# Decode kernel with cached attention: keys brought in by transposing DMAs in place of TensorE transposes and copies

## The chip, the cores and the metric

The kernel runs on one core of a Trainium2 chip. The metric is the device time of one execution in microseconds (us). Beside it the profile has a span, from the first to the last recorded instruction, and names of engines: PE is TensorE, with PEld for its weight loads, DVE is VectorE, ACT is ScalarE, POOL is GpSimd, and SP is SyncE, which issues all the DMAs of this kernel.

## The reference

Four sequences (B = 4) decode one token each through the same two layers twice: attention over cached keys and values, and a gated MLP. Keys and values have 8 heads of 4096 rows of 128 bf16 numbers; each key head serves 4 query heads.

```python
def _A_ref(x, k_cache, v_cache, wq, wo):
    q = (x @ wq).reshape(B, 1, 32, 128).transpose(0, 2, 1, 3)
    k = repeat(k_cache, 4, axis=1); v = repeat(v_cache, 4, axis=1)
    p = softmax(einsum("bhqd,bhkd->bhqk", q, k) * 128 ** -0.5)
    o = einsum("bhqk,bhkd->bhqd", p, v)
    return o.transpose(0, 2, 1, 3).reshape(B, 1, 4096) @ wo
def _B_ref(x, w_gate, w_up, w_down):
    return (gelu(x @ w_gate) * (x @ w_up)) @ w_down
x = x + _A_ref(layernorm(x), k_cache, v_cache, wq, wo)
x = x + _B_ref(layernorm(x), w_gate, w_up, w_down)
x = x + _A_ref(layernorm(x), k_cache, v_cache, wq, wo)
x = x + _B_ref(layernorm(x), w_gate, w_up, w_down)
```

Both attention layers use the same caches and weights. The caches are 33.6 MB each, the weights 13.9 MB.

## The kernel before

The loop at line 371 goes over the four sequences ("batches"). In a batch the first attention layer, its MLP and the scores of the second attention layer are computed; the second layer's values for that batch follow in the next batch's turn, beside the next batch's keys. So keys are read from HBM once per batch, and values twice. The last batch's second-layer values, and the last MLP for all four batches together, form the tail after the loop (lines 470 to 488).

Keys: keys(b, kvh) at line 253 fills one of 8 resident tiles kt (pool ktp, 1 MB each, head dimension on the partitions), which stay until the second layer's scores of the batch have read them. It loads two raw tiles k_t of 512 KB through load_kv (line 124; a ring of 6 buffers, KV_BUFS, that keys and values share), turns every 128 x 128 block on PE (line 262, 32 to a head) into a PSUM tile tp, and evac (line 246) copies each group of 8 blocks to kt, two copies of five on ACT (line 249), three on DVE (line 251).

Scores: scores (line 270) multiplies the queries, placed in a sparse tile zq, with the resident keys, 8 matmuls a head (line 276), and collects 4 heads in one PSUM tile sc. softmax (line 281) works on such a group of 4 heads with DVE, POOL and ACT, and turn (line 305) transposes its result pr to pT. set_queries (line 161) puts the queries of a batch into zq.

Values: values (line 315) loads two tiles v_t of 512 KB for a head and multiplies them with pT (line 328); its finish transposes the result back (line 337), and DVE writes it to OT_bf (lines 342 and 343). out_proj (line 184) multiplies by wo.

Order: tc.manual_schedule (line 349) keeps the instructions of PE and SP as they are written. Both engines take their instructions in that order, so an SP instruction that waits holds every DMA written after it. In the loop, V(kvh, p) is a value head of the first layer, W() one of the second layer of the batch before (an "old" head), and O() the finish of the oldest head still open. Before the change the order of a batch is: keys 0; turns of the old softmaxes (batch 0: the second half of wq and the q projection); keys 1 to 7, with the scores of head k written after the keys of head k+1, two old heads after the scores of heads 1 and 2, the softmax of heads 0 to 3 after the scores of head 3, and values 0 to 2 between keys 6, keys 7 and the last scores; the softmax of heads 4 to 7; values 3; an old head; then values 4 to 7 with the output projection, and the norms, the MLP (ffn, line 202) and the q projection of the second layer with the other five old heads between their steps; last the second layer's scores, line 465 on, head by head, with their softmaxes. Batch 0 also loads wo before values 3 (line 429) and the three MLP weights after values 7 (line 448).

Of the kernel before, what the change touches and what calls it, by code (L numbers as in the profile page):

```python
# [9 lines left out]
BF16 = mybir.dt.bfloat16  # L10
# [5 lines left out]
P = 128  # L16
# [3 lines left out]
CH = 16  # L20
TB = 8
GH = 4
# [5 lines left out]
def kernel(  # L28
# [16 lines left out]
    nc = tc.nc  # L45
    B, Sq, D = A_x.shape
    _, Hkv, Sk, Dh = A_k_cache.shape
# [8 lines left out]
    NT = C // CH  # L56
    NKB = 8
    NCC = C // NKB
    CT = NCC // NT
# [8 lines left out]
    ktp = ctx.enter_context(tc.tile_pool(name="ktp", bufs=Hkv))  # L68
# [11 lines left out]
    ident_bf = const.tile([P, P], BF16, name="ident_bf")  # L80
# [42 lines left out]
    def load_kv(cache, b, kvh, t, name):  # L123
        tl = kvin.tile([P, CH, Dh], BF16, name=name, tag="kv")
        rows = slice(t * CH * P, (t + 1) * CH * P)
        dq.dma_start(out=tl[:], in_=cache[b, kvh, rows].rearrange("(p c) d -> p c d", p=P))  # L126
        return tl
# [33 lines left out]
    def set_queries(z, b):  # L161
        nc.vector.tensor_copy(out=z[:, :, ZP:ZP + rep],
                              in_=q1_bf[:, b].rearrange("p (k h) -> p k h", h=rep))

    def q_proj(b0, nb, dst, parts):
        bs = slice(b0, b0 + nb)
        hp = Hq // parts
        for part in range(parts):
            qps = ps_misc.tile([P, nb, hp], FP32, name="qps", tag="misc")
            for i in range(hp):  # L170
                m = part * hp + i
                for k in range(KD):
                    nc.tensor.matmul(qps[:, :, i], lhsT=wq_sb[:, k, m * Dh:(m + 1) * Dh],  # L173
                                     rhs=xn_bf[:, bs, k], start=(k == 0), stop=(k == KD - 1))
            if nb == 1:
                nc.vector.tensor_copy(
                    out=dst(part, hp),
                    in_=qps.rearrange("p o (k h) -> p (o k) h", h=rep))
            else:
                nc.vector.tensor_copy(out=dst(part, hp), in_=qps[:])  # L180
# [60 lines left out]


    KT = {}
    evac_ctr = [0]

    def evac(out_ap, in_ap):
        evac_ctr[0] += 1
        if evac_ctr[0] % 5 in (1, 3):
            nc.scalar.copy(out=out_ap, in_=in_ap)  # L249
        else:  # L250
            nc.vector.tensor_copy(out=out_ap, in_=in_ap)  # L251

    def keys(b, kvh):

        kt = ktp.tile([P, NKB, NCC, P], BF16, name="kt", tag="kt")
        KT[kvh] = kt
        for t in range(NT):
            kn = load_kv(A_k_cache, b, kvh, t, "k_t")
            for g in range(CH // TB):
                tp = ps_tp.tile([P, TB // CT, CT, P], BF16, name="tp", tag="tp")  # L260
                for i in range(TB):
                    nc.tensor.transpose(tp[:, i // CT, i % CT, :], kn[:, g * TB + i, :],  # L262
                                        ident_bf[:, :])
                k0 = g * TB // CT
                evac(kt[:, k0:k0 + TB // CT, t * CT:(t + 1) * CT, :], tp[:])

    def new_scores():
        return ps_sc.tile([P, NCC * P], FP32, name="sc", tag="sc")
# [1 line left out]
    def scores(sc, kvh, zq):  # L270

        s = kvh % GH
        for kbp in range(2):
            off = ZP - rep * (2 * s + kbp)
            for j in range(4):
                nc.tensor.matmul(sc[32 * j:32 * j + 32, :], lhsT=zq[:, kvh, off:off + 32],  # L276
                                 rhs=KT[kvh][:, 2 * j + kbp].rearrange("p c k -> p (c k)"),
                                 start=(s == 0 and kbp == 0), stop=(s == GH - 1 and kbp == 1),
                                 skip_group_check=True)

# [24 lines left out]
    def turn(soft):  # L305

        pr, rden = soft
        ptp = ps_tp.tile([P, NCC, P], BF16, name="ptp", tag="tp")
        for cc in range(NCC):
            nc.tensor.transpose(ptp[:, cc, :], pr[:, cc, :], ident_bf[:, :])  # L310
        pT = pTp.tile([P, NCC, P], BF16, name="pT", tag="pT")
        nc.vector.tensor_copy(out=pT[:], in_=ptp[:])
        return pT, rden

    def values(b, kvh, prob, o_bf):

        pT, rden = prob
        s = kvh % GH  # L320
        ot = ps_ot.tile([P, 2, 2 * Dh], FP32, name="ot", tag="ot")
        for t in range(NT):
            v = load_kv(A_v_cache, b, kvh, t, "v_t").rearrange(
                "p (j b c) d -> p j c b d", j=4, b=2, c=CT)
            for cl in range(CT):
                cc = t * CT + cl
                for j in range(4):
                    nc.tensor.matmul(  # L328
                        ot[32 * j:32 * j + 32, 0].rearrange("p (b d) -> p b d", b=2),
                        lhsT=pT[:, cc, 32 * j:32 * j + 32], rhs=v[:, j, cl],  # L330
                        start=(cc == 0), stop=(cc == NCC - 1))
        os = osp.tile([P, 2, Dh], FP32, name="os", tag="os")
        nc.scalar.copy(out=os.rearrange("p b d -> p (b d)"), in_=ot[:, 0])  # L333

        def finish():
            for k in range(2):
                nc.tensor.transpose(ot[:, 1, k * P:(k + 1) * P], os[:, k, :], ident_f[:, :])  # L337
            od = grp.tile([P, rep], FP32, name="od", tag="od")

            src = ot[:, 1, 8 * s:]  # L340
            sel = bass.AP(src.tensor, src.offset, [src.ap[0], [1, rep], [132, 2], [32, 4]])
            nc.vector.tensor_reduce(out=od[:], in_=sel, axis=AX.XY, op=ALU.add)  # L342
            nc.vector.tensor_tensor(out=o_bf[:, b, kvh * rep:(kvh + 1) * rep], in0=od[:],  # L343
                                    in1=rden[:, s], op=ALU.mult)

        return finish
# [24 lines left out]
    for b in range(B):  # L371
        z1 = zq1[b % 2]
        old = list(range(Hkv)) if b > 0 else []
        rest = []

        def V(kvh, prob):
            rest.append(values(b, kvh, prob, OT_bf))

        def W():
            if old:  # L380
                kvh = old.pop(0)
                rest.append(values(b - 1, kvh, prob2[kvh // GH], OT2_bf))

        def O():
            if rest:
                rest.pop(0)()

        if b > 0:
            set_queries(z1, b)
        sc = new_scores()  # L390
        keys(b, 0)
        if b == 0:
            dq.dma_start(out=wq_sb[:, :, hq0:], in_=wq_dram[:, :, hq0:])
            q_proj(0, B, lambda part, hp: q1_bf[:, :, part * hp:(part + 1) * hp], 4)
            set_queries(z1, 0)
        else:
            prob2 = [turn(soft2[0])]
        keys(b, 1)
        if b > 0:
            prob2.append(turn(soft2[1]))  # L400
        scores(sc, 0, z1)
        keys(b, 2)
        scores(sc, 1, z1)
        W()
        keys(b, 3)
        O()
        scores(sc, 2, z1)
        W()
        keys(b, 4)
        O()  # L410
        scores(sc, 3, z1)
        soft1 = softmax(sc)
        sc = new_scores()
        keys(b, 5)
        p0 = turn(soft1)
        scores(sc, 4, z1)
        V(0, p0)
        keys(b, 6)
        O()
        scores(sc, 5, z1)  # L420
        V(1, p0)
        keys(b, 7)
        O()
        scores(sc, 6, z1)
        V(2, p0)
        scores(sc, 7, z1)
        soft1 = softmax(sc)
        if b == 0:
            dma_weights("wo")
        V(3, p0)  # L430
        O()
        W()
        O()
        p1 = turn(soft1)
        V(4, p1)
        O()
        out_proj(b, 1, OT_bf, range(0, 4))
        V(5, p1)
        O()
        out_proj(b, 1, OT_bf, [4])  # L440
        V(6, p1)
        O()
        out_proj(b, 1, OT_bf, [5])
        V(7, p1)
        O()
        out_proj(b, 1, OT_bf, [6])
        if b == 0:
            dma_weights("wg", "wu", "wd")
        W()
        O()  # L450
        out_proj(b, 1, OT_bf, [7])
        for _ in ffn(b, 1):
            W()
            O()
        for _ in layer_norm(b, 1):
            W()
            O()
        while old:
            W()
            O()  # L460
        q_proj(b, 1, lambda part, hp: zq2[:, part * GH:(part + 1) * GH, ZP:ZP + rep], 2)
        while rest:
            O()
        soft2 = []
        for g in range(2):
            sc = new_scores()
            for s in range(GH):
                scores(sc, g * GH + s, zq2)
            soft2.append(softmax(sc))
# [49 lines left out]
```

## Time and profile before

| | us |
|---|---|
| two runs of the kernel before | 386.70 and 391.99, median 389.35 |
| the profiled execution | 388.58 |
| its span | 386.8 |

The mean granted clock of TensorE in the profiled execution is 0.706 of full speed. From the groups of instructions, beside those that are shown further down:

| line, engine, what | count | busy us |
|---|---|---|
| 328 PE, values | 1024 | 61.0 |
| 337 PE, turning the results back | 128 | 39.9 |
| 276 PE, scores of the second layer | 256 | 23.4 |
| 333 ACT, copying the results | 64 | 23.8 |
| 192 PE, output projection | 640 | 21.4 |

A group's row has the line, the engine, the operation, out<-in with shapes, the count, then busy us and mean ns of one, then the idle time before them on their engine and what ended it. A row of the timeline has the start and the length in us, the engine and the line, and the number of instructions that were merged; a bracket tells how long the engine had stood idle before and what released it. Matmuls overlap, so the lengths of PE rows that follow each other overlap too, and starts are the safer guide. A row of the DMA issues has the number of DMAs, the KB of one (1 KB is 1024 bytes; MB are millions of bytes), and the us from issue to landing. Windows show for each stretch the busy time of every engine, the granted clock and what the DMA engines did.

### The profile page before, as it was taken

Reading aid. Unit: us, or ns where it says so; the run is one execution under the profiler, and the core shown is the slowest. Engines: PE = TensorE matmul, PEld = TensorE weight load, DVE = VectorE, ACT = ScalarE, POOL = GpSimd, SP = SyncE. Lnnn points to the kernel's source line nnn. Section 1 sums busy time; section 2 is a strip of 40 time slices with the busy share of each in tenths; the row PEclk is TensorE's granted clock in tenths of the full one; section 3 lists DMA queues with packets and bytes.
Section 4 is the critical chain, followed back from the end, with each engine's and each line's share of the span. In section 5 each row is a group of like instructions: output and inputs, shape, how many; then the busy total and the mean of one; then the engine's idle time right before and its main releaser. Section 6 shows DMA issues by size and latency. Waiting matters only on the chain.

```text
span 386.8 us, 11139 instructions
## 1 busy us (share of the span) xinstructions
PE 277.7 (72%) x4900; PEld 198.9 (51%) x4900; DVE 135.7 (35%) x528; ACT 90.0 (23%) x154; POOL 14.0 (4%) x38
## 2 busy tenths in 40 slices
PE   0699704845987868879967577878967688796855
PEld 0686602645566525565755345664745355553535
DVE  0546411132454421341735211434653213313132
ACT  1236310100353411100634311101644211002100
POOL 0000000000100000000100000001000000001000
PEclk9999875555798965555989955557999655556555
DMA  7989999996189999970698999861899999704900
GB/s 284 407 314 341 380 350 408 403 374 252 55 288 407 363 407 407 401 290 3 228 402 309 366 403 352 339 219 55 282 410 406 409 395 382 276 8 156 386 5 2
DMA packets 35745, 115.29 MB, mean 298 GB/s; under 512 B 3176, under 2 KB 9072, under 8 KB 35696
## 3 DMA queue, kind: packets, MB, share of 16 engines
q1 hardware_dynamic: 35696, 114.58, 78.6%
q8 instruction: 38, 0.62, 0.6%
q14 instruction: 11, 0.09, 0.1%
HBM read 114.56 MB, written 0.00 MB: 296 GB/s over the span
## 4 chain that ended last, share of the span: by engine, by line
PE 47%; DMA 25%; DVE 15%; issue 6%; ACT 3%; SPq 2%; POOL 2%; DVEq 0%; POOLq 0%; ACTq 0%
DMA k_t<-in_A_k_cache_dram 10%; PE ot L328 10%; DMA v_t<-in_A_v_cache_dram 10%; PE tp L262 9%; PE ot L337 7%; PE sc L276 6%; DMA wd_sb<-in_B_w_down_dram 5%; PE qps L173 5%; PE yT L192 4%; ACT pr L294 2%; PE hg L210 2%; PE hu L227 2%; DVE kt L251 2%; SPq L126 2%; DVE od L342 2%
## 5 line engine op out<-in xcount | busy, mean ns | idle before, releaser
L262 PE MATMUL tp<-ident_bf,k_t 128*128 128x128 bf16 x1024 | 74.1, 232 | 16.4 <-DMA k_t<-in_A_k_cache_dram 10.9
L328 PE MATMUL ot<-v_t,pT 128*32 128x256 bf16 x1024 | 61.0, 371 | 32.7 <-DMA v_t<-in_A_v_cache_dram 26.3
L262 PEld LDWEIGHTS <-k_t 128*128 128x128 bf16 x1024 | 65.6, 105 | 29.7 <-DMA k_t<-in_A_k_cache_dram 15.6
L251 DVE COPY kt<-tp 128x1024 bf16<-128x1024 bf16 x76 | 51.3, 688 | 50.8 <-PE tp L262 50.2
L249 ACT COPY kt<-tp 128x1024 bf16<-128x1024 bf16 x52 | 52.3, 1012 | 59.8 <-PE tp L262 59.6
L328 PEld LDWEIGHTS <-pT 128*32 128x32 bf16 x1024 | 28.9, 116 | 50.1 <-DMA v_t<-in_A_v_cache_dram 19.1
L333 ACT COPY os<-ot 128x256 f32<-128x256 f32 x64 | 23.8, 372 | 132.5 <-PE ot L328 132.5
L342 DVE TENSOR_REDUCE od<-ot 128x4 f32<-128x32 f32 x64 | 12.0, 187 | 93.9 <-PE ot L337 93.6
L337 PE MATMUL ot<-ident_f,os 128*128 128x128 f32 x128 | 39.9, 412 | 2.1 <-ACT os L333 2.1
L192 PEld LDWEIGHTS <-wo_sb 128*128 128x128 bf16 x640 | 23.0, 107 | 16.7 <-issue 16.3
L192 PE MATMUL yT<-OT_bf,wo_sb 128*128 128x1 bf16 (+1 forms) x640 | 21.4, 166 | 10.8 <-DVE OT_bf L343 10.7
L337 PEld LDWEIGHTS ot<-ident_f,os 128*128 128x128 f32 x128 | 17.5, 192 | 21.2 <-issue 16.4
L173 PE MATMUL qps<-xn_bf,wq_sb 128*128 128x1 bf16 (+1 forms) x640 | 18.9, 166 | 12.0 <-DVE xn_bf L157 10.1
L294 ACT ACTIVATE pr<-sc,nb 128x512 bf16<-128x512 f32 x16 | 11.0, 688 | 69.3 <-DVE am L290 67.7
L173 PEld LDWEIGHTS <-wq_sb 128*128 128x128 bf16 x640 | 18.1, 104 | 12.8 <-DVE xn_bf L157 10.5
L276 PE MATMUL sc<-kt,zq_128 128*32 128x512 bf16 x256 | 23.4, 545 | 0.0
L283 DVE TENSOR_REDUCE m<-sc 128x1 f32<-128x512 f32 x16 | 11.0, 689 | 20.4 <-PE sc L276 20.3
L288 POOL PARTITION_ALL_REDUCE gm<-am x16 | 6.2, 388 | 301.2 <-DVE am L285 301.2
L276 PEld LDWEIGHTS <-zq_128 128*32 128x32 bf16 x256 | 8.5, 131 | 13.9 <-issue 12.4
L210 PE MATMUL hg<-xn_bf,wg_sb 128*128 128x1 bf16 (+1 forms) x280 | 8.3, 166 | 8.0 <-DVE xn_bf L157 8.0
L210 PEld LDWEIGHTS <-wg_sb 128*128 128x128 bf16 x280 | 7.9, 104 | 9.4 <-DVE xn_bf L157 6.7
L310 PE MATMUL ptp<-ident_bf,pr 128*128 128x128 bf16 x64 | 7.4, 248 | 6.4 <-ACT pr L294 6.1
(118 smaller groups left out, 157.5 us busy)
## 6 DMA issues: line engine op xcount, KB each, us to landing
v_t<-in_A_v_cache_dram SPq DMA_DIRECT2D x128, 512.0 KB, 6.3
k_t<-in_A_k_cache_dram SPq DMA_DIRECT2D x64, 512.0 KB, 6.2
wq_sb<-in_A_wq_dram SPq DMA_DIRECT2D x2, 2048.0 KB, 10.8
wo_sb<-in_A_wo_dram SPq DMA_DIRECT2D x1, 4096.0 KB, 19.5
wg_sb<-in_B_w_gate_dram SPq DMA_DIRECT2D x1, 1792.0 KB, 11.2
wu_sb<-in_B_w_up_dram SPq DMA_DIRECT2D x1, 1792.0 KB, 15.4
wd_sb<-in_B_w_down_dram SPq DMA_DIRECT2D x1, 1792.0 KB, 20.1
x_bf<-in_A_x_dram SPq DMA_DIRECT2D x1, 4.0 KB
```

Of the source, the lines that this page charges most:

```text
L173: nc.tensor.matmul(qps[:, :, i], lhsT=wq_sb[:, k, m * Dh:(m + 1) * Dh], rhs=xn_bf[:, bs, k], start=(k == 0), stop=(k == KD - 1))
L192: nc.tensor.matmul(OP["y"][:, :, dk], lhsT=wo_sb[:, i, dk * P:(dk + 1) * P], rhs=o_bf[:, bs, i], start=(i == 0 and dk == 0), stop=(i == Hq ...
L210: nc.tensor.matmul(hg[:, m, :], lhsT=wg_sb[:, k, m * P:(m + 1) * P], rhs=xn_bf[:, bs, k], start=(k == 0), stop=(k == KD - 1))
L249: nc.scalar.copy(out=out_ap, in_=in_ap)
L251: nc.vector.tensor_copy(out=out_ap, in_=in_ap)
L262: nc.tensor.transpose(tp[:, i // CT, i % CT, :], kn[:, g * TB + i, :], ident_bf[:, :])
L276: nc.tensor.matmul(sc[32 * j:32 * j + 32, :], lhsT=zq[:, kvh, off:off + 32], rhs=KT[kvh][:, 2 * j + kbp].rearrange("p c k -> p (c k)"), st ...
L294: nc.scalar.activation(out=pr.rearrange("p c k -> p (c k)"), in_=sc[:], func=ACT.Exp, bias=nb[:, 0:1], scale=scale, accum_out=ls[:])
L328: nc.tensor.matmul(ot[32 * j:32 * j + 32, 0].rearrange("p (b d) -> p b d", b=2), lhsT=pT[:, cc, 32 * j:32 * j + 32], rhs=v[:, j, cl], star ...
L333: nc.scalar.copy(out=os.rearrange("p b d -> p (b d)"), in_=ot[:, 0])
L337: nc.tensor.transpose(ot[:, 1, k * P:(k + 1) * P], os[:, k, :], ident_f[:, :])
L342: nc.vector.tensor_reduce(out=od[:], in_=sel, axis=AX.XY, op=ALU.add)
```

## The change

keys no longer loads raw tiles, turns and copies them. It issues one transposing DMA from SP for a head, from the cache in HBM to the resident tile. The 4096 rows of a head are viewed as 256 rows of 16 consecutive keys (2048 elements); the DMA writes, for each of the 16 keys in such a row, a run of 256 elements in each of the 128 partitions. So the tile has the shape 128 x 16 x 256 in place of 128 x 8 x 4 x 128, a new helper kcols picks the 512 columns for a matmul of the scores, and the index of the chunk of pT in values goes from t * CT + cl to cl * NT + t to match. The raw tiles k_t, the transposes of line 262 and evac are gone; the 6 buffers of load_kv serve values alone.

The order of a batch changes with it. All eight key DMAs are issued first (in batch 0 the second half of wq behind the first of them), then the q projection of batch 0 or the turns of the old softmaxes, set_queries, the scores of all heads with the two softmaxes, and only then value heads. No old head stands ahead of value head 7 now; in batches 1 to 3 all eight come from there on, three of them between the second norm and the q projection. wo stays between values 2 and 3.

```diff
     KT = {}
-    evac_ctr = [0]
-
-    def evac(out_ap, in_ap):
-        evac_ctr[0] += 1
-        if evac_ctr[0] % 5 in (1, 3):
-            nc.scalar.copy(out=out_ap, in_=in_ap)
-        else:
-            nc.vector.tensor_copy(out=out_ap, in_=in_ap)
 
     def keys(b, kvh):
 
-        kt = ktp.tile([P, NKB, NCC, P], BF16, name="kt", tag="kt")
+
+        kt = ktp.tile([P, CH, Sk // CH], BF16, name="kt", tag="kt")
         KT[kvh] = kt
-        for t in range(NT):
-            kn = load_kv(A_k_cache, b, kvh, t, "k_t")
-            for g in range(CH // TB):
-                tp = ps_tp.tile([P, TB // CT, CT, P], BF16, name="tp", tag="tp")
-                for i in range(TB):
-                    nc.tensor.transpose(tp[:, i // CT, i % CT, :], kn[:, g * TB + i, :],
-                                        ident_bf[:, :])
-                k0 = g * TB // CT
-                evac(kt[:, k0:k0 + TB // CT, t * CT:(t + 1) * CT, :], tp[:])
+        dq.dma_start_transpose(out=kt[:], in_=A_k_cache[b, kvh].rearrange("(r s) d -> r (s d)", s=CH))
+
+    def kcols(kvh, kb):
+        return KT[kvh][:, CT * kb:CT * (kb + 1), :].rearrange("p s r -> p (s r)")
...
-                                 rhs=KT[kvh][:, 2 * j + kbp].rearrange("p c k -> p (c k)"),
+                                 rhs=kcols(kvh, 2 * j + kbp),
...
-                cc = t * CT + cl
+                cc = cl * NT + t
                 for j in range(4):
                     nc.tensor.matmul(
                         ot[32 * j:32 * j + 32, 0].rearrange("p (b d) -> p b d", b=2),
                         lhsT=pT[:, cc, 32 * j:32 * j + 32], rhs=v[:, j, cl],
-                        start=(cc == 0), stop=(cc == NCC - 1))
+                        start=(t == 0 and cl == 0), stop=(t == NT - 1 and cl == CT - 1))
...
-        if b > 0:
-            set_queries(z1, b)
+        for kvh in range(Hkv):
+            keys(b, kvh)
+            if b == 0 and kvh == 0:
+                dq.dma_start(out=wq_sb[:, :, hq0:], in_=wq_dram[:, :, hq0:])
+        if b == 0:
+            q_proj(0, B, lambda part, hp: q1_bf[:, :, part * hp:(part + 1) * hp], 4)
+        else:
+            prob2 = [turn(sf) for sf in soft2]
+        set_queries(z1, b)
         sc = new_scores()
...
+        for kvh in range(GH):
+            scores(sc, kvh, z1)
         soft1 = softmax(sc)
         sc = new_scores()
-        keys(b, 5)
+        scores(sc, 4, z1)
         p0 = turn(soft1)
-        scores(sc, 4, z1)
+        for kvh in range(5, 8):
+            scores(sc, kvh, z1)
+        soft1 = softmax(sc)
         V(0, p0)
-        keys(b, 6)
-        O()
-        scores(sc, 5, z1)
         V(1, p0)
-        keys(b, 7)
-        O()
-        scores(sc, 6, z1)
+        O()
         V(2, p0)
-        scores(sc, 7, z1)
-        soft1 = softmax(sc)
+        O()
         if b == 0:
             dma_weights("wo")
         V(3, p0)
         O()
-        W()
-        O()
         p1 = turn(soft1)
+        O()
         V(4, p1)
-        O()
         out_proj(b, 1, OT_bf, range(0, 4))
+        O()
         V(5, p1)
```

More of the change, by code (lines that the diff above doesn't have):

```diff
@@ L386, in O @@
                 rest.pop(0)()
-        if b > 0:
-            set_queries(z1, b)
-        sc = new_scores()
[L391 to L403, printed above, removed]
-        W()
-        keys(b, 3)
-        O()
-        scores(sc, 2, z1)
-        W()
-        keys(b, 4)
-        O()
-        scores(sc, 3, z1)
+        for kvh in range(Hkv):
[7 more added lines that the diff above has]
+        set_queries(z1, b)
+        sc = new_scores()
+        for kvh in range(GH):
+            scores(sc, kvh, z1)
         soft1 = softmax(sc)
         sc = new_scores()
-        keys(b, 5)
+        scores(sc, 4, z1)
         p0 = turn(soft1)
-        scores(sc, 4, z1)
+        for kvh in range(5, 8):
+            scores(sc, kvh, z1)
+        soft1 = softmax(sc)
         V(0, p0)
-        keys(b, 6)
+        V(1, p0)
         O()
-        scores(sc, 5, z1)
-        V(1, p0)
-        keys(b, 7)
-        O()
-        scores(sc, 6, z1)
-        V(2, p0)
-        scores(sc, 7, z1)
-        soft1 = softmax(sc)
+        V(2, p0)
+        O()
         if b == 0:
@@ L431 @@
         O()
-        W()
+        p1 = turn(soft1)
         O()
-        p1 = turn(soft1)
         V(4, p1)
+        out_proj(b, 1, OT_bf, range(0, 4))
         O()
-        out_proj(b, 1, OT_bf, range(0, 4))
         V(5, p1)
```

## The prediction

> **What bounds the kernel now.** I read the page from its first part to its chain, then cut the span into stages, then went through one batch on the queues of SP and PE. The page first:
>
> ```profile
> span 386.8 us, 11139 instructions
> PE 277.7 (72%) x4900; PEld 198.9 (51%) x4900; DVE 135.7 (35%) x528; ACT 90.0 (23%) x154; POOL 14.0 (4%) x38
> ...
> PEclk9999875555798965555989955557999655556555
> ...
> GB/s 284 407 314 341 380 350 408 403 374 252 55 288 407 363 407 407 401 290 3 228 402 309 366 403 352 339 219 55 282 410 406 409 395 382 276 8 156 386 5 2
> ...
> q1 hardware_dynamic: 35696, 114.58, 78.6%
> ...
> PE 47%; DMA 25%; DVE 15%; issue 6%; ACT 3%; SPq 2%; POOL 2%; DVEq 0%; POOLq 0%; ACTq 0%
> ```
>
> No engine fills the span. In the slices the DMA runs at about 407 GB/s for long stretches and falls to 55, 3, 55 and 8 once in each batch. The chain is nearly half PE and a quarter DMA. So it is neither bytes alone (114.58 MB at 408 GB/s would be 281 us) nor PE alone, but stages that hand over to each other. Stages, by windows (columns: stretch, length, busy time and count for PE, PEld, DVE, ACT, POOL, then granted clock, DMA share, GB/s):
>
> ```profile
> 50.00:58.00 8.00, 0.00 (x0) 0.00 (x0) 0.67 (x4) 0.78 (x2) 0.69 (x2) 0.72 1.09 350
> 58.00:68.00 10.00, 5.04 (x65) 3.02 (x66) 1.42 (x7) 0.74 (x2) 0.00 (x0) 0.50 1.03 407
> ...
> 145.00:158.00 13.00, 10.87 (x202) 7.61 (x202) 1.78 (x10) 1.86 (x5) 0.00 (x0) 0.50 1.03 408
> ...
> 177.90:186.00 8.10, 7.71 (x89) 3.60 (x90) 3.29 (x12) 1.62 (x3) 1.22 (x3) 0.67 0.00 0
> 186.00:212.00 26.00, 20.75 (x322) 15.55 (x325) 13.75 (x34) 12.75 (x18) 1.27 (x3) 0.93 0.92 341
> ...
> 342.00:387.00 45.00, 30.40 (x519) 19.21 (x518) 11.96 (x59) 4.79 (x13) 1.66 (x4) 0.54 0.31 118
> ```
>
> A batch has three stages. Keys come in and are turned by PE (186 to 212: PE 80% busy, DMA only 341 GB/s). Then values stream at 408. Then a chain of norms, MLP and projections ends in the second layer's scores, and there the DMA stands at 0. The marks of the batches are those scores (x64):
>
> ```profile
> 97.13 5.69 PE L276 MATMUL sc<-kt,zq_128 128*32 128x512 bf16 x64
> ...
> 177.82 6.30 PE L276 MATMUL sc<-kt,zq_128 128*32 128x512 bf16 x64
> ...
> 342.11 6.08 PE L276 MATMUL sc<-kt,zq_128 128*32 128x512 bf16 x64
> ```
>
> From 97.13 to 342.11 are three batches of 81.7 us. Before the first mark stand 97.1 us, after the last 44.7.
>
> **The change, part by part.** What goes, and what is lost with it:
>
> ```profile
> L262 PE MATMUL tp<-ident_bf,k_t 128*128 128x128 bf16 x1024 | 74.1, 232 | 16.4 <-DMA k_t<-in_A_k_cache_dram 10.9
> ...
> L251 DVE COPY kt<-tp 128x1024 bf16<-128x1024 bf16 x76 | 51.3, 688 | 50.8 <-PE tp L262 50.2
> L249 ACT COPY kt<-tp 128x1024 bf16<-128x1024 bf16 x52 | 52.3, 1012 | 59.8 <-PE tp L262 59.6
> ...
> k_t<-in_A_k_cache_dram SPq DMA_DIRECT2D x64, 512.0 KB, 6.2
> ```
>
> 1024 transposes (74.1 us of PE), 128 copies (51.3 us of DVE, 52.3 of ACT) and 64 loads of 512 KB go. In come 32 transposing DMAs of 1 MB (1.049 MB in the page's units, 256 rows of 4 KB). Call the time of one in a full queue t. The rest of the sum has rows.
>
> A loss comes with it. Before, raw keys could go into the six kv buffers ahead of time:
>
> ```profile
> 160.68 9.75 SPq L126 DMA_DIRECT2D k_t<-in_A_k_cache_dram  x6
> ```
>
> These six were issued 17 us before the mark, while the chain ran. The new key DMAs write the resident tiles, which the second layer's scores still read. So SP waits for scores of head 0 and the values of the next batch queue behind it on SP. The 3 MB of prefetch (7.7 us at 408) are gone, and the keys of a batch now stand bare: PE has turns and its first scores to do meanwhile, but no values, because the three old heads that ran before value head 4 now come at the end.
>
> A batch after the change, from mark to mark. Rows:
>
> ```profile
> v_t<-in_A_v_cache_dram SPq DMA_DIRECT2D x1, 512.0 KB, 3.2
> ```
> ```profile
> 143.94 1.04 PE L328 MATMUL ot<-v_t,pT 128*32 128x256 bf16 x16 [0.52 <-DVE pT L312]
> ...
> 149.91 1.05 PE L328 MATMUL ot<-v_t,pT 128*32 128x256 bf16 x16
> 150.89 0.69 PE L337 MATMUL ot<-ident_f,os 128*128 128x128 f32 x2
> 152.11 0.56 PE L192 MATMUL yT<-OT_bf,wo_sb 128*128 128x1 bf16 x16 [0.53 <-DVE OT_bf L343]
> 152.61 1.05 PE L328 MATMUL ot<-v_t,pT 128*32 128x256 bf16 x16
> ...
> 170.43 0.43 PE L135 MATMUL st<-X_122,mean_f 128*128 128x8 f32 x2
> 173.38 1.87 PE L173 MATMUL qps<-xn_bf,wq_sb 128*128 128x1 bf16 x64 [2.52 <-DVE xn_bf L157]
> ```
>
> - Head 0 of the second scores frees its tile after 6.30/8 = 0.8 us. The first bytes take 1.9 us more: the lone load (3.2 us to landing, DMA idle before it, from the window 100 to 105) less its 0.524 MB at 408 (1.29). Together 2.7.
> - Eight key DMAs: 8t. Scores, softmax and turns ride along, the last head's 0.8 us under the first values.
> - Value heads 0 to 4, ten loads: 12.9 us at 408. PE needs 2.7 us a head even with its projection (149.91 to 152.61), against 2.6 of DMA, so up to here the DMA leads. Head 4's matmul effectively begins 0.5 before the last load lands: 12.4.
> - From head 4 to the mark the order is that of before, 143.94 to 177.82 = 33.9 us. Three old heads (1.6 each: 0.98 from 149.91 to 150.89, and the 0.69 behind it less its overlap) move between the last norm and the q projection: +4.8. They cover that norm's wait of 2.52 (row 173.38): -2.5. So 36.2. The DMA needs 41.1 us for the 32 loads and has 48.6, so PE leads here; all at the clock 0.50 that these rows had, thus no further loss for a colder PE. If six buffers don't keep it fed, each late load costs up to 1.3 us.
> - Sum: 2.7 + 8t + 12.4 + 36.2 = 51.3 + 8t.
>
> Batch 0 becomes DMA-bound to the landing of the last weights:
>
> ```profile
> wq_sb<-in_A_wq_dram SPq DMA_DIRECT2D x2, 2048.0 KB, 10.8
> wo_sb<-in_A_wo_dram SPq DMA_DIRECT2D x1, 4096.0 KB, 19.5
> ...
> wd_sb<-in_B_w_down_dram SPq DMA_DIRECT2D x1, 1792.0 KB, 20.1
> ```
> ```profile
> 1.15 0.41 SPq L353 DMA_DIRECT2D wq_sb<-in_A_wq_dram  x1
> ```
> ```profile
> 87.95 1.65 PE L235 MATMUL yT_1285<-H_bf,wd_sb 128*128 128x1 bf16 x56 [2.97 <-DMA wd_sb<-in_B_w_down_dram]
> ```
>
> Start 3.0 (issue at 1.15, first bytes 1.9). wq 4.19 MB: 10.3. Keys 8t. Then wo and wd (6.03 MB in pieces of 1 KB, at the 350 of 50 to 58): 17.2; values, and gate and up, which are as large as wd (12.06 MB at 408): 29.6. From that landing to the mark 97.13 - 87.95 = 9.2. Sum 69.3 + 8t. The tail has no keys in it, and its DMA share of 0.31 leaves it to PE and DVE: 44.7 as before.
>
> ```profile
> L162 DVE COPY zq_0_126<-q_bf 128x32 bf16<-128x32 bf16 x2 | 0.3, 171 | 0.0
> ```
> ```profile
> 351.32 0.61 PE L310 MATMUL ptp<-ident_bf,pr 128*128 128x128 bf16 x4 [2.49 <-ACT pr L294]
> ```
>
> The moves of set_queries (0.17 us), of the q projection of batch 0 and of the second softmax ahead of the values cost nothing: they lie under the landing keys and values. Without that cover a softmax would show as it does in the tail, where PE waits 2.49 us for one, up to twice a batch. The wq half stays behind key 0 and wo between value heads 2 and 3, so these queues see no new order.
>
> **Span = 69.3 + 8t + 3(51.3 + 8t) + 44.7 = 267.9 + 32t.** Now t, which no row shows. From below: a plain load, 1.049 MB at 408 GB/s, t = 2.57; a reason to be faster than plain loads in 4 KB pieces is not to be seen, since the same bytes go through the same 16 engines. From above: a DMA that does not overlap with its neighbour, 2.57 + 1.9 = 4.47, or one that moves in 256-byte pieces, 4.70 (below). I take 350 GB/s, t = 3.00, the slowest rate of a full queue in this trace (window 50 to 58, 1 KB pieces): each row of 4 KB is contiguous in HBM, which speaks for the fast end, but its write side has to scatter to 128 partitions. That gives 363.9, and with the 1.8 us that the profiled execution has around its span (388.58 against 386.8) 366. The profiled execution is 0.2% under the median 389.35, so the sum stands to it as to the median.
>
> The trace's best is 408 GB/s for plain loads. By the Trainium skill, Advanced Engine Details and Errata, section X-Bar Transpose (TRN2), transposing DMAs are about as fast as regular ones, with 350 to 400 GB/s expected, some 90% of a copy; as an estimate 90% of 408 would be t = 2.86 and 361 us. No run here shows it yet.
>
> **The rivals.**
>
> Short pieces, slower. The crossbar may move a key row as sixteen pieces of 256 bytes rather than one of 4 KB. The trace prices pieces: 1 KB at 350 GB/s is 46.8 ns on each of 16 engines, 4 KB at 408 is 160.6; that is 8.9 ns a piece and 37.9 ns a KB, so 256 bytes take 18.4 ns, 223 GB/s, t = 4.70, and 418.3 + 1.8 = 420 us. For it: 128 columns of bf16 are 256 bytes. Against: the source view makes rows of 2048 contiguous elements. The Trainium skill, DMA: Bandwidth & Descriptors, section Latency and other measured facts, gives 261 GB/s for a transposing DMA with a non-contiguous middle dimension and 350 to 400 for a contiguous one; by the former t would be 4.02 and the time 398, an estimate.
>
> No overlap, slower. If a transposing DMA starts only when the one before has landed, each pays the 1.9 us: t = 4.47, 410.9 + 1.8 = 413 us. For it: nothing in the trace. Against: plain loads overlap (6.2 us to landing, 1.3 us apart).
>
> Either one decides from its point on: the span stays at 386.8 when t = (386.8 - 267.9)/32 = 3.72, which is 282 GB/s.
>
> No difference. The prefetch that is lost and the bare keys eat what PE gains, t between 3.47 and 3.96 (2% each way): 381 to 396 us, in the middle 389. For it: the stage that PE now turns in still gets 341 GB/s, so little is won there if the crossbar is slower than that.
>
> **How the numbers follow.** Two runs of before lie 1.4% apart, so about 2% is what can be told from no change. Chances: t up to 3.47 (the forecast, 352 to 381) 0.53; the middle 0.13; short pieces 0.15; no overlap 0.12; something slower than both 0.07. Faster 0.53, same 0.13, slower 0.34. The range goes from 348 (t = 2.57 gives 352, less 4 for value heads that come earlier than I let them) to 420 (short pieces); outside lie the 0.07 and some 0.1 at its two ends. The likeliest case alone has 348 to 381.
>
> **What would show it.** Right: no tp rows; 32 key DMAs; in each batch some 24 us (8t) at 350 GB/s with PE nearly idle; marks about 75 us apart, the first near 93, 44.7 after the last; DMA at 0 for some 7 us around each mark. Wrong: marks over 81 us apart with a rate below 282 GB/s while keys land (short pieces if the DMA share stays full, no overlap if it has a hole per DMA); or values that land late though the keys came fast, then the six buffers are the error.

## The result and the profile after

The changed kernel takes 443.0 us (442.44 and 443.56) against 389.35: 1.138 times as long, with a 95% interval of 1.104 to 1.172. The prediction was 366 us, 348 to 420, faster with a chance of 0.53. It was wrong in sign and missed the range by 23 us.

The page of the changed kernel, first its totals, the GB/s of the 40 slices, the DMA queue and the packets, and the chain:

```profile
span 440.7 us, 8879 instructions
PE 235.9 (54%) x3876; PEld 140.4 (32%) x3876; DVE 87.5 (20%) x452; ACT 38.7 (9%) x102; POOL 13.9 (3%) x38
...
GB/s 255 309 215 190 265 375 374 404 383 23 138 224 202 206 399 407 409 271 43 219 205 224 287 413 406 353 184 107 205 208 222 370 411 393 294 359 17 387 91 2
DMA packets 158614, 115.13 MB, mean 261 GB/s; under 512 B 134248, under 2 KB 140144, under 8 KB 158576
...
q1 hardware_dynamic: 158576, 114.58, 87.7%
...
DMA 31%; PE 30%; SPq 25%; DVE 6%; ACT 4%; issue 3%; POOL 1%; ACTq 0%; DVEq 0%; POOLq 0%
```

PE, DVE and ACT lost the work that was to go (ACT 90.0 to 38.7 us). PE fell from 277.7 to 235.9, by less than the 74.1 us of the transposes, for what stayed took longer at a mean granted clock of 0.657, 0.706 before: a matmul of the values 408 ns in the mean, 371 before. The bytes are the same, yet the DMA queue is in use for 87.7% of a span that is 14% longer, and a quarter of the chain is now SP's queue. The slices show where: at 190 to 225 GB/s in each batch, where keys come in.

The marks of the batches, from the timeline of PE (start, length, the 64 scores matmuls of the second layer):

```profile
111.29 5.36 PE L264 MATMUL sc<-kt,zq_128 128*32 128x512 bf16 x64
...
206.77 5.40 PE L264 MATMUL sc<-kt,zq_128 128*32 128x512 bf16 x64
...
396.24 6.23 PE L264 MATMUL sc<-kt,zq_128 128*32 128x512 bf16 x64
```

The first mark came at 111.3 (before 97.1), then three batches of 95.0 each (before 81.7), and 44.5 after the last (before 44.7). So the loss is 14 us in the first stretch and 13 in each batch. One batch by windows: the keys, value heads 0 to 4, and from head 4 to the next mark.

```profile
112.40:154.60 42.20, 12.39 (x124) 4.08 (x117) 5.54 (x21) 2.33 (x6) 2.48 (x6) 0.61 1.08 202
154.60:167.60 13.00, 8.69 (x84) 3.94 (x83) 3.10 (x14) 2.27 (x6) 0.83 (x2) 0.50 1.02 410
167.60:206.80 39.20, 32.47 (x648) 22.81 (x652) 10.13 (x62) 4.68 (x13) 0.00 (x0) 0.50 0.77 292
```

Eight key heads take 42 us at 202 GB/s with the DMA share at 1.08: in the mean the queue is full and slow, not empty (steps of 0.25 us, below, show short holes in it). The values behind them run at 410 on the same queue. On SP's timeline the eight key DMAs hold the queue for 5.0 us each here, and for 4.9 in the next two batches:

```profile
112.38 40.16 SPq L250 DMA_TRANSPOSE kt<-in_A_k_cache_dram  x8
152.60 42.82 SPq L126 DMA_DIRECT2D v_t<-in_A_v_cache_dram  x32
```

### The profile page after: what moved, and what is told of

It is laid out like the page before. It is cut to its first block, busy times and chain, and to the rows that moved or that the text cites. A ratio compares the mean times of both kernels' runs of the same rounds, so it can differ in the third digit from the quotient of the medians.

```text
span 440.7 us, 8879 instructions
## 1 busy us (share of the span) xinstructions
PE 235.9 (54%) x3876; PEld 140.4 (32%) x3876; DVE 87.5 (20%) x452; ACT 38.7 (9%) x102; POOL 13.9 (3%) x38
## 2 busy tenths in 40 slices
DMA packets 158614, 115.13 MB, mean 261 GB/s; under 512 B 134248, under 2 KB 140144, under 8 KB 158576
## 3 DMA queue, kind: packets, MB, share of 16 engines
q1 hardware_dynamic: 158576, 114.58, 87.7%
## 4 chain that ended last, share of the span: by engine, by line
DMA 31%; PE 30%; SPq 25%; DVE 6%; ACT 4%; issue 3%; POOL 1%; ACTq 0%; DVEq 0%; POOLq 0%
SPq L250 22%; DMA v_t<-in_A_v_cache_dram 18%; PE ot L316 9%; DMA kt<-in_A_k_cache_dram 9%; PE ot L325 6%; DMA wd_sb<-in_B_w_down_dram 5%; PE sc L264 4%; PE qps L173 3%; ACT os L321 2%; SPq L126 2%; PE yT L192 2%; PE hg L210 2%; PE hu L227 1%; ACT pr L282 1%; PE ptp L298 1%
## 5 line engine op out<-in xcount | busy, mean ns | idle before, releaser
L316 PE MATMUL ot<-v_t,pT 128*32 128x256 bf16 x1024 | 70.2, 408 | 32.4 <-DMA v_t<-in_A_v_cache_dram 29.6
L325 PE MATMUL ot<-ident_f,os 128*128 128x128 f32 x128 | 43.5, 444 | 19.1 <-ACT os L321 19.1
L316 PEld LDWEIGHTS <-pT 128*32 128x32 bf16 x1024 | 30.2, 119 | 56.7 <-issue 32.7
L264 PE MATMUL sc<-kt,zq_1_127 128*32 128x512 bf16 x128 | 16.3, 604 | 51.0 <-DMA kt<-in_A_k_cache_dram 51.0
L264 PE MATMUL sc<-kt,zq_0_126 128*32 128x512 bf16 x128 | 16.3, 603 | 48.6 <-DMA kt<-in_A_k_cache_dram 48.1
L325 PEld LDWEIGHTS ot<-ident_f,os 128*128 128x128 f32 x128 | 18.7, 204 | 44.0 <-ACT os L321 36.8
L264 PEld LDWEIGHTS <-zq_1_127 128*32 128x32 bf16 x128 | 3.8, 108 | 60.7 <-issue 49.8
L264 PE MATMUL sc<-kt,zq_128 128*32 128x512 bf16 x256 | 23.1, 539 | 0.0
L264 PEld LDWEIGHTS <-zq_0_126 128*32 128x32 bf16 x128 | 3.9, 108 | 58.1 <-issue 52.0
L298 PE MATMUL ptp<-ident_bf,pr 128*128 128x128 bf16 x64 | 8.6, 277 | 12.1 <-ACT pr L282 12.0
L264 PEld LDWEIGHTS <-zq_128 128*32 128x32 bf16 x256 | 8.5, 130 | 12.7 <-issue 11.0
L298 PEld LDWEIGHTS <-pr 128*128 128x128 bf16 x64 | 5.5, 123 | 18.4 <-ACT pr L282 14.8
```

The source lines that it names most:

```text
L316: nc.tensor.matmul(ot[32 * j:32 * j + 32, 0].rearrange("p (b d) -> p b d", b=2), lhsT=pT[:, cc, 32 * j:32 * j + 32], rhs=v[:, j, cl], star ...
```

## The experiments

Three questions: what makes a transposing DMA take 5.0 us a head, what else the prediction had wrong, and whether such a DMA pays anywhere. Where nothing else is said, a time is that of a single run; the kernel before took 385 to 389 us beside these, and single runs of it between 384 and 392, so steps of a few us between two kernels mean little unless a trace bears them out.

**The crossbar or the order.** (Crossbar is the word here for a DMA's own way of transposing.) The key DMA as a plain one, all else and every wait unchanged; the keys then stay untransposed, so only the time counts:

```diff
-        dq.dma_start_transpose(out=kt[:], in_=A_k_cache[b, kvh].rearrange("(r s) d -> r (s d)", s=CH))
+        dq.dma_start(out=kt.rearrange("p (t c) r -> p t (c r)", t=2),
+                     in_=A_k_cache[b, kvh].rearrange("(t p s) d -> p t (s d)", t=2, s=CH))
```

> The changed kernel with one edit: each key head comes by one plain 1 MB DMA in 4 KB pieces into its resident tile, so the keys are not transposed there and the scores are those of untransposed blocks; all other work and every wait is the same. Theory A (the crossbar DMA itself is slow: about 5.0 us for a head where a plain one takes 2.57): the span falls by 32 x 2.4 = 78 to about 362 us, time 364. Rival (the loss is the new order and the lost prefetch): it stays over 389 us.

367.95 us, beside 386.39. The change without the crossbar, that is the new order, the lost prefetch and PE free of the transposes, is thus a gain as long as the keys come at the rate of a plain load (409 GB/s in its key stage, 99 to 116). What turns it into a loss of 54 us is the transposing DMA: 443 less 368 is 75 us, 2.3 us for each of the 32 heads.

**Pieces.** A plain DMA again, now in pieces of 256 bytes:

```diff
-        dq.dma_start_transpose(out=kt[:], in_=A_k_cache[b, kvh].rearrange("(r s) d -> r (s d)", s=CH))
+        dq.dma_start(out=kt.rearrange("p c (h d) -> p (c h) d", d=Dh),
+                     in_=A_k_cache[b, kvh].rearrange("(c p) d -> p c d", p=P))
```

> As the plain-DMA kernel, but in pieces of 256 bytes (one key row to one partition, 32 rows to each); keys again not transposed, the rest the same. Theory A1 (a transposing DMA is slow since it moves 256-byte pieces at the 291 GB/s seen inside one, 3.6 us a head, and on top loses 1.4 us at the end of each DMA, when the rate falls to nearly nothing before the next begins): plain 256-byte pieces overlap at their ends, so about 3.6 us a head, span 396, time 398. Rival A2 (256-byte pieces cost about 20 ns each on an engine, the dips are only unevenness): 5.0 us a head, time 443 as with the crossbar. Rival A3 (it is the crossbar, pieces don't matter): 2.6 us a head, time 364.

440.95 us, within 0.5% of the crossbar's 443.0 which is the number of the rival A2. The packets of the plain 4 KB kernel, and of this one, and the key stage of this one (20 us of it, last column GB/s):

```profile
DMA packets 35222, 115.13 MB, mean 315 GB/s; under 512 B 2664, under 2 KB 8560, under 8 KB 35184
```
```profile
DMA packets 59798, 115.13 MB, mean 262 GB/s; under 512 B 2664, under 2 KB 41328, under 8 KB 59760
```
```profile
122.00:142.00 20.00, 4.72 (x36) 1.29 (x36) 2.02 (x7) 0.78 (x2) 0.83 (x2) 0.50 1.06 216
```

216 GB/s in a full queue, with no crossbar in it: a plain DMA that reads pieces of 256 bytes is as slow as this. Its packets are not that small. 41328 under 2 KB are 32768 more than the 8560 of the plain 4 KB kernel, 1024 for each of 32 heads, so 1 KB or four pieces each; contiguous pieces of 1 KB had 350 GB/s in the trace before. The crossbar's packets are: 134248 under 512 bytes are 131584 more than the 2664 of a kernel with as many plain DMAs, 4112 for each of 32 heads, and 4096 of them are the 256-byte rows of a head. So both kernels read 256 bytes at a time, but they don't move them in the same way, and the equal times don't show the same cause. The rates in time differ too, here 18 us of the plain kernel (124 to 142) in steps of 0.45:

```profile
GB/s 232 218 218 218 218 216 205 48 191 275 275 250 216 218 218 216 221 173 223 246 223 223 214 221 216 218 214 218 155 244 241 232 214 218 218 218 218 216 214 171
```

**A cost for each DMA.** Inside a transposing DMA the rate is 290, then falls away, as these 10 us of the changed kernel in steps of 0.25 show, with the share of the DMA engines in tenths above:

```profile
DMA  9599907999999999943899500389999999999973
GB/s 242 134 75 139 25 6 141 291 289 291 289 291 291 291 289 291 290 91 75 190 231 160 2 0 11 36 174 290 292 290 288 292 291 290 290 292 287 291 152 84
```

The plain pieces flow evenly near 218; the crossbar runs at 290 and has holes. At 290 a head would take 1.049 MB / 290 GB/s = 3.6 us. So of the 2.4 us by which 5.0 exceeds a plain load's 2.57, 1.0 belongs to the rate inside and 1.4 to the stretches below it. I took the holes for the end of one DMA. So each DMA was cut in two of 128 rows:

```diff
-        dq.dma_start_transpose(out=kt[:], in_=A_k_cache[b, kvh].rearrange("(r s) d -> r (s d)", s=CH))
+        kr = A_k_cache[b, kvh].rearrange("(r s) d -> r (s d)", s=CH)
+        for h in range(2):
+            dq.dma_start_transpose(out=kt[:, :, h * P:(h + 1) * P], in_=kr[h * P:(h + 1) * P])
```

> The changed kernel with each head's transposing DMA cut in two of 512 KB (128 rows each). Theory A1 (1.4 us lost at the end of each DMA): 32 more ends, +45 us, about 488. Rival A2 (only bytes or pieces count): no change, 443. In between if the loss at an end grows with the size of the DMA.

444.0 us. There is no fixed cost of 1.4 us for each end; my theory fell, and with it the rival of the prediction that let DMAs wait for each other. A loss that goes with the bytes of a DMA is not excluded. Nor is it settled whether SP or the DMA engines set this pace: SP works on the eight transposing DMAs almost without a break (40.16 us of the 42.20). It issues the eight of the plain 4 KB kernel, as large, in 6.54 us (row below), far ahead of their bytes, which take 20.6; but the eight with 256-byte pieces, in a queue that is evenly full, hold it for 34.1 us too.

```profile
93.03 6.54 SPq L250 DMA_DIRECT2D kt<-in_A_k_cache_dram  x8
```

**The view of the source.** The same bytes as 4096 rows of 128, as 1024 of 512 and as 128 of 4096 elements, where the change has 256 of 2048:

```diff
-        dq.dma_start_transpose(out=kt[:], in_=A_k_cache[b, kvh].rearrange("(r s) d -> r (s d)", s=CH))
+        dq.dma_start_transpose(out=kt.rearrange("p (o s) r -> p o (s r)", o=1), in_=A_k_cache[b, kvh])
```

> The changed kernel with the source of the transposing DMA viewed as 4096 rows of 128 elements (256 bytes) in place of 256 rows of 2048; the resident columns then have another order, so scores and values pair other rows; all amounts are the same. If the pieces are 256 bytes in either view (the trace's packets say so): no change, 443 us. If the contiguous 4 KB rows did help: slower by some 30% of the key time, 32 x 1.5 = 48 us, about 490.

> The changed kernel with the source of the transposing DMA viewed as 1024 rows of 4 keys (512 elements), between the 256 rows of 2048 elements (5.0 us a head) and the 4096 rows of 128 (4.3 us). The order of the resident columns changes, so scores and values pair other rows; amounts are the same. Theory (pieces of 256 bytes in any view, and what differs is how far apart in HBM the pieces lie that are read together: 4 KB, 1 KB, 256 bytes): between the two, 425 to 440. Rival (only the fully contiguous view is better): 443.

> As before, with 128 rows of 32 keys (4096 elements, 8 KB apart). Theory (distance in HBM): at least as slow as with 4 KB, 443 to 470. Rival (longer contiguous rows help): under 440. The order of the resident columns changes, so scores and values pair other rows; amounts are the same.

420.43, 423.67 and 447.11 us. With 1, 4, 16 and 32 column groups of 128 in a row, the time is 420, 424, 443, 447, all with the same 134248 packets under 512 bytes: the contiguous 4 KB row, on which the prediction leaned, is the wrong way round. In the key stage the first has 253 GB/s and the changed kernel 205:

```profile
122.00:142.00 20.00, 5.76 (x44) 1.57 (x44) 2.02 (x7) 0.78 (x2) 0.83 (x2) 0.50 1.20 253
```
```profile
122.00:142.00 20.00, 4.72 (x36) 1.27 (x36) 2.02 (x7) 0.78 (x2) 0.83 (x2) 0.50 1.14 205
```

Is it the distance of the pieces in HBM, or the number of groups? Sixteen DMAs of 64 KB a head, once with pieces 4 KB apart and once side by side, were to tell:

> The changed kernel with each head's DMA cut into 16 of 64 KB, one for each of the 16 column groups, so that each reads 256 pieces of 256 bytes that lie 4 KB apart; same data to the same places. Theory (distance in HBM): the same stream as the uncut DMA if an instruction costs nothing by itself, 443; at least 15 us over the kernel with 16 near DMAs in any case. Rival (distance doesn't matter, the order of the groups does): equal to the kernel with 16 near DMAs.

> As the kernel with 16 far DMAs, same count and size, but each reads 256 consecutive keys, pieces of 256 bytes side by side; the order of the resident columns changes, so scores and values pair other rows. Theory (distance in HBM): as with the view of 4096 rows, 420, if an instruction costs nothing by itself; at least 15 us under the far kernel in any case. Rival: equal to the far kernel.

936.73 and 936.49 us. This told nothing on the distance, but showed another limit, on SP's timeline of the far kernel:

```profile
228.77 164.86 SPq L252 DMA_TRANSPOSE kt<-in_A_k_cache_dram  x128
```

SP takes 164.86/128 = 1.29 us for each of these, and 64 KB in 1.29 us is 51 GB/s. So the distance was changed alone, with whole DMAs of 1 MB and one group:

```diff
-        dq.dma_start_transpose(out=kt[:], in_=A_k_cache[b, kvh].rearrange("(r s) d -> r (s d)", s=CH))
+        b2, i = b - b % 2, kvh + Hkv * (b % 2)
+        far = A_k_cache[b2:b2 + 2].rearrange("b h (r s) d -> (b h r) (s d)", s=CH)
+        dq.dma_start_transpose(out=kt.rearrange("p (o s) r -> p o (s r)", o=1),
+                               in_=far[:, i * Dh:(i + 1) * Dh])
```

> The changed kernel with 32 transposing DMAs of 1 MB, each of one column group: 4096 pieces of 256 bytes that lie 4 KB apart, taken from 16 heads of two batches; over two batches every byte is read once. The keys so come to the wrong heads; amounts are the same. Theory (distance in HBM): 4 KB apart costs what it costs in the changed kernel, about 443. Rival (the number of column groups in a DMA does it, one here, one in the view of 4096 rows, 16 in the change): 420.

424.47 us, close to the rival's 420 and 19 us under the changed kernel, though the pieces lie as far apart as there. So the distance is not the cause. The time goes with the number of column groups in a DMA, or with what changes along with it: a group has 4096, 1024, 256 and 128 rows in the four views, and that was not varied alone. It is no fixed price for a group either, since the cut in halves doubled the groups that SP issues and took 444.0. Why groups cost is open, and so is what makes the holes.

**The finishes.** The last stretch of a batch took 39.2 us instead of the 36.2 forecast. The waits of PE in it, 167.6 to 206.8, us in total, times, longest:

```profile
PE ot L325 <- ACT os L321: 5.8, 11, 0.5
```

The order before has no such wait between head 4 and the mark. There a finish was that of the head before; the changed order finishes the head just multiplied, and waits 0.53 us for ACT's copy each time.

```diff
         p1 = turn(soft1)
-        O()
         V(4, p1)
+        O()
         out_proj(b, 1, OT_bf, range(0, 4))
-        O()
         V(5, p1)
```

> The changed kernel with one finish less at the turn of the second probabilities, so that from value head 4 on each finish is that of the head before and not of the head just multiplied. Theory (each finish now waits 0.53 us for ACT's copy of its own head, some ten times between head 4 and the mark, which the order of before did not do): 3.6 to 5.8 us a batch less over three batches, 442 becomes 425 to 431. Rival (these waits lie beside others, the value loads above all): no change, 442.

436.06 us, -7 against the median of the change: the theory's sign, half its size. The batches went from 95.0 to 93.0 us. The waits for ACT are gone, but PE now meets others in the same stretch:

```profile
PE yT L192 <- DVE OT_bf L331: 2.1, 4, 0.5
PE ot L316 <- DMA v_t<-in_A_v_cache_dram: 1.2, 2, 0.6
PE ot L316 <- DVE od L330: 0.8, 1, 0.8
PE hg L210 <- DVE xn_bf L157: 0.8, 1, 0.8
```

The first of these, 2.1 us, the order of before has too, in the stretch from head 4 to its mark; the changed order had traded it for the 5.8. So less than 5.8 was to be won back.

**The lost prefetch.** Value heads 0 to 2 loaded ahead of the keys:

```diff
-            v = load_kv(A_v_cache, b, kvh, t, "v_t").rearrange(
+            v = (VT.pop((kvh, t), None) or load_kv(A_v_cache, b, kvh, t, "v_t")).rearrange(
...
+        if b > 0:
+            for i in range(KV_BUFS):
+                VT[i // NT, i % NT] = load_kv(A_v_cache, b, i // NT, i % NT, "v_t")
         for kvh in range(Hkv):
             keys(b, kvh)
```

> As the kernel with one finish less, and in batches 1 to 3 the loads of value heads 0 to 2 are written on SP ahead of the key DMAs, so that they run while DMA is idle around the mark. Theory (the prefetch that the change lost is worth what heads 0 to 4 wait for their loads, 12.4 us against some 8 of PE work, up to the whole 7.7 us of six loads): 4 to 7.7 us a batch less than without it, that is 12 to 23 us. Rival (the loads only change places with the keys): no change against the kernel with one finish less.

428.76 us, 7.3 less than the kernel with one finish less, and not 12 to 23. The batches went from 93.0 to 90.8 us. The six loads do run around the mark, but then hold the only six buffers until the last key has landed, so value head 3 can't load beside the keys. DMA stands still there, and PE waits. The stretch 145 to 165 of this kernel, then PE's first half of head 3:

```profile
GB/s 290 152 288 146 81 67 221 290 291 289 290 55 0 0 0 0 0 90 328 434 377 401 385 98 180 229 360 385 393 410 393 418 442 418 426 401 410 451 401 385
```
```profile
160.40 0.40 PE L318 MATMUL ot<-v_t,pT 128*32 128x256 bf16 x8 [1.98 <-DMA v_t<-in_A_v_cache_dram]
```

**Where it pays.** The kernel before has its DMA at or near 0 for some 8 us from each of its first three marks. A transposing DMA costs too much elsewhere, but there nothing is in its way. So the order of before, with one head of eight by a transposing DMA:

```diff
+    def cross(b, kvh):
+        kt = ktp.tile([P, CH, Sk // CH], BF16, name="kt", tag="kt")
+        KT[kvh] = kt.rearrange("p (k c) (t q) -> p k t c q", c=CT, t=NT)
+        dq.dma_start_transpose(out=kt[:], in_=A_k_cache[b, kvh].rearrange("(r s) d -> r (s d)", s=CH))
...
         keys(b, 2)
+        cross(b, 3)
```

> The kernel before with its order, PE transposes and copies for seven heads, and head 3 alone by a transposing DMA, issued behind the raw loads of head 2. Theory (the DMA stands idle for some 8 us around the mark, and a transposing DMA that costs 5.0 in place of 2.6 us fits in there, while PE is relieved of 32 transposes, 2 us, in its fullest stage): 1 to 5 us a batch less, 372 to 384 against 386 to 389. Rival (the 2.4 us more of DMA show in each batch, for the loads queued behind come later): 389 to 396.

> As the kernel with head 3 by a transposing DMA, and head 5 too, issued right behind it. Theory: the second no longer fits into the idle time, so its 2.4 us of DMA stand against 2 us of PE saved: within 4 us of the kernel with head 3 alone, either way. Rival (PE is what bounds the stage throughout): again 1 to 5 us a batch less.

377.75 us with one head and 397.0 with two, beside 385.41. The first fits into the idle time: the value loads written behind it start 7.6 us after the mark (181.63, mark at 174.01), and 7.3 after it in the kernel before (185.15, mark at 177.82). A batch takes 78.5 us against 81.7; how much of that comes from the 32 transposes fewer on PE, and how much from the megabyte that moved into idle time, was not separated. The second does not fit and costs far more than its own 2.4 us a batch, against the expectation: two DMAs hold SP for 8.51 us, and the value loads behind them start 11.9 us after the mark. Of the 19 us between the two kernels 7 fall before the first mark (103.4 against 96.3), the rest into the batches; that was not taken apart further. The first row is of the kernel with one head, the others of that with two:

```profile
181.63 3.99 SPq L126 DMA_DIRECT2D v_t<-in_A_v_cache_dram  x4
```
```profile
185.35 4.97 PE L285 MATMUL sc<-kt,zq 128*32 128x512 bf16 x64
```
```profile
188.64 8.51 SPq L258 DMA_TRANSPOSE kt<-in_A_k_cache_dram  x2
197.25 2.71 SPq L126 DMA_DIRECT2D v_t<-in_A_v_cache_dram  x4
```

Two more versions with one head were run several times beside the kernel before (median 387.03 us): the view of 4096 rows for it, and head 0 in place of head 3.

> The kernel before with head 3 alone by a transposing DMA, its source now viewed as 4096 rows of 128 elements, the scores of that head reading their columns with a stride of 16 elements. Theory (0.7 us less for each of four such DMAs, partly in idle time; the stride costs PE nothing): 375 to 378. Rival (the strided reading slows PE's 32 scores matmuls of that head a batch): above 380.

> The kernel before with head 0 alone by a transposing DMA: raw keys of heads 1 to 3 are loaded ahead, the DMA of head 0 behind them, and the scores run 1, 2, 3, 0. Its tile is the first that the second layer's scores give back, 2.4 us before that of head 3. Theory (the DMA starts that much earlier in its idle time): 371 to 376, against 378 with head 3. Rival (what bounds is not the start of this DMA): 378.

The first has 387.31 us, a ratio of 1.003 (0.999 to 1.006). The better view leaves the columns with a stride of 16, and PE pays for that: the eight scores matmuls of that head take 2.00 us where those of head 2, without the stride, take 0.61 in the same kernel, both at a granted clock of 1.00:

```profile
200.06 2.00 PE L285 MATMUL sc<-kt,zq 128*32 128x512 bf16 x8
```
```profile
194.98 0.61 PE L285 MATMUL sc<-kt,zq 128*32 128x512 bf16 x8
```

In all, the scores matmuls of this kernel are busy for 51.2 us, those of the kernel with head 3 and no stride for 42.3. These 8.9 us are about what lies between 387.31 and 377.75.

The second has 376.85 us, a ratio of 0.970 (0.962 to 0.978): faster than the kernel before, and no better than the 377.75 of head 3. This did not test the theory, for the DMA did not start earlier, as the marks and SP's rows show, head 0's kernel first, then head 3's:

```profile
177.29 5.31 PE L285 MATMUL sc<-kt,zq 128*32 128x512 bf16 x64
```
```profile
180.96 4.00 SPq L258 DMA_TRANSPOSE kt<-in_A_k_cache_dram  x1
```
```profile
174.01 5.19 PE L285 MATMUL sc<-kt,zq 128*32 128x512 bf16 x64
```
```profile
177.53 4.01 SPq L258 DMA_TRANSPOSE kt<-in_A_k_cache_dram  x1
```

3.7 us after the mark the one, 3.5 the other. In both, PE's first signal after the mark comes with the 32nd of the 64 matmuls, the last of heads 0 to 3, which ends at 180.9 and 177.5; SP starts right behind it. So head 0's tile came back no earlier than head 3's, while in the changed kernel PE signals after each head, and SP starts 1.1 us after the mark (112.38).

## Why the prediction was wrong, point by point

- **t, the time of one key DMA, is the step that failed.** I bounded it by 2.57 and 4.70 and took 3.00, "the slowest rate of a full queue in this trace", since contiguous rows of 4 KB spoke for the fast end. It measured 5.0, above both ends: 32 x 2.0 = 64 of the 77 us between 366 and 443. The runs show two parts of it: inside a DMA the rate is 290 GB/s and not the 350 that I took, and the stretches below that add 1.4 us a head. The rival of short pieces had the size of a piece right, 256 bytes, which contiguous rows did not change; I gave it 0.15 because I took the shape of the source view for the size of a piece, and no row showed that. Its price, 223 GB/s or 4.70 us, was right for plain pieces (216), and came near the crossbar's 202 to 213 by luck: the same 256-byte packets run at 290 inside a DMA and at 205 or 253 in the key stage, depending on the view. So pieces alone don't set the price, and what does is open. Even that rival's 420 us would have been low, by 32 x 0.3 for t and by the finishes below.
- **The sign that was to tell the rivals apart** could not: the DMA share stays full in the mean (1.08), as for short pieces, and there is a deep hole about every 5 us, as for no overlap. The DMAs cut in two decided against no overlap.
- By the Trainium skill, Advanced Engine Details and Errata, section X-Bar Transpose (TRN2), the transposing DMA should have been as fast as a regular one, at 350 to 400 GB/s. The measurement decides: here it ran at 202 to 253, where plain loads reach 408 to 410. The 261 GB/s that the Trainium skill gives in DMA: Bandwidth & Descriptors, section Latency and other measured facts, is near the best view's 253, but that page ties it to a non-contiguous middle dimension, and here the contiguous long rows were the slower ones.
- **"From head 4 to the mark the order is that of before" was false.** The order of the heads is, that of the finishes is not. 39.2 us against 36.2; with 0.6 more up to head 4 some 3.6 a batch, about 11 us in all. The kernel with one finish less won 2.0 a batch of it back.
- **Right:** the rest of the sum. From mark to mark 2.7 + 8t + 13.0 + 39.2, with the measured stages and t = 5.02 (40.16/8 on SP), is 95.1, where 206.77 - 111.29 is 95.5. Value heads 0 to 4 took 13.0 us (forecast 12.4), the tail 44.5 (44.7), and the first mark came at 111.3, where 69.3 + 8t gives 109.3 for t = 5.0. With a plain load in place of the crossbar the sum gives 350 + 2 us and the three batches' 3.6 add 11: 363, and 368 was measured; the last 5 us were not taken apart.
- **The point from which it is a loss** was given as t = 3.72 with the order as I had it. With the measured order it lies lower: from 368 us at 2.57 to 387 are 19 us, 0.6 for each of 32, so about 3.2. Even the best view, 0.7 us a head less ((443.0 - 420.4)/32, so 4.3), is beyond it.

## What to carry to other kernels

The price of a kind of DMA that no row shows is the first thing to measure: one transposing DMA in a run would have given its packets (256 bytes, whatever the row of the view), its rate inside and its holes, before a queue that is already 79% full was given 32 of them. A price worked out from another kind of DMA is a guess even where it comes near. Where the DMA stands idle anyway, one transposing DMA a batch took 3% off the same kernel that eight of them, with a new order, made 14% slower. When a change reorders work, check the order of the small steps (here which head a finish belongs to) as closely as that of the large ones.

## What was not expected of the hardware

- A transposing DMA with 1, 4, 16 or 32 groups of 128 columns in a row made the kernel 420, 424, 443 and 447 us long with the same bytes, and the distance of the pieces in HBM made at most some 4 us of it (424 against 420, single runs).
- Its rate inside is flat at 290 GB/s and falls to nearly 0 in between; cutting it in two changed nothing (444.0 against 443.0).
- SP needs 1.29 us to issue one of 64 KB, while the DMA stands idle between them (51 GB/s).
- Packets of the same size, 1 KB, came at 350 GB/s where a piece was 1 KB and at 216 where four pieces of 256 bytes made one packet.
- Eight matmuls that read their columns with a stride of 16 took 2.00 us, and 0.61 without it at the same clock.
- The page's count of bytes read from HBM leaves the transposed keys out, though the queue's own count (114.58 MB) has them; the changed kernel, then the one before:

```profile
HBM read 81.01 MB, written 0.00 MB: 184 GB/s over the span
```
```profile
HBM read 114.56 MB, written 0.00 MB: 296 GB/s over the span
```
